# Turning two more attention chunks with VectorE and regrouped data in place of TensorE transposes

## The chip, the cores and the metric

The kernel runs on one core of a Trainium2 chip. The metric is the device time of one execution in microseconds (us); the time before is the median of three runs. All data is fp32.

The core's engines are named as in the profile: PE (TensorE: matmuls and transposes, weight loads shown apart as PEld), DVE (VectorE), ACT (ScalarE), POOL (GpSimd) and SP (SyncE, which here issues nearly all DMA transfers). Each engine runs its own instructions in order and waits on semaphores for the others.

## The reference

Two parts, one behind the other. First a linear attention with decay, on q, k and v of 4 batches x 8 heads x 768 tokens x 64, in blocks of 64 tokens:

```
for b in range(nb):                       # blocks of 64 tokens
    intra = einsum('bhic,bhjc->bhij', qb, kb) * Dmask
    intra = einsum('bhij,bhjd->bhid', intra, vb)
    inter = einsum('bhid,bhde->bhie', qb * lam_pow, kv_state)
    out[block] = intra + inter
    kv_state = lam**64 * kv_state + einsum('bhsd,bhse->bhde', kb * rev_pow, vb)
```

Its output, as 3072 tokens x 512, is the input x of a dense mixture of four experts: `out = sum over e of p[:, e] * (relu(x @ w1[e]) @ w2[e])`, with w1 of 512 x 1024, w2 of 1024 x 512, and p the probabilities of the tokens, normalised.

## The kernel before

**Tiling.** A chunk is 128 tokens of all 8 heads of one batch, so there are 24 chunks; eight make a group, and the three groups of 1024 tokens are the unit of the second part. The products with w1 and w2 are done by a scheme of seven products in place of eight (M1 to M7), partly nested, with sums of operands made by POOL and DVE. A pair (group, expert) is a unit; the twelve units run one behind the other.

**Stages.** At first chunks 0 to 7 go through attention, mixed with the first product of unit (0, 0). Then the main loop runs over the units. Each has seven products, and each product eight places x, so that the work of the loop has a step number, `(at * 7 + i) * 8 + x`. In the part of the trace that matters here a product takes some 13 us, a step some 1.6 us, and step 0 stands at about 87 us. At every step the loop emits some matmuls of the second product of one unit (`q<-w2t,m`, L1254) and of the first product of the next (`pg<-xs,...`, L1195), with the evictions from PSUM to SBUF behind them on DVE (`m<-pg,m`) and ACT (L1208, L1172, L1176); then it takes one or two pieces of deferred work from lists, runs what attention has due at that step, and pumps the chores of POOL (`w1o`, `ops`: the sums for the operands of later products, and their stores).

**Attention in the loop.** Chunks 8 to 23 go through attention in the loop. The schedule is written out by hand: `AT` lists the step at which each chunk's scores are made (34 for chunk 8, 40 for 9, 48 for 10), and `attention()` (L911 and on) derives all other steps from it: the loads, the turn, and `values` of the chunk before.

The scores need q and k turned, with the head dimension on the partitions. There are two ways to it.

- *On PE* (`turn`, L732 and on; chunks 0 to 9): q and k are loaded as they lie, in two half DMAs each (L178); eight PE transposes of 128x128 (L745) put them into two PSUM banks; ACT copies them to SBUF (L753 q, L754 k). The step is 4 before the scores, the load 7 before that.
- *Across* (`turn_across`, from L719; chunks 10 to 23): k is loaded in one DMA (L174), and ACT regroups it in 16 copies of 32x128 (`regroup`, L526), handed out two per step by the list `moves`. q is regrouped in DRAM: `bring_across` (L488) copies it from DRAM to the DRAM tensor `across` in 64 pieces with runs of 128 B, sent one per call of `trickle`, and `load_across` brings one chunk of it to SBUF in one DMA. Two DVE transposes of 128x512 (L725; each turns the 32x32 blocks in place) do the rest. They aren't issued at once, but put in the list `lately`, from which the loop takes at its steps. The turn is 7 steps before the scores, the load of q 5 before the turn, that of k `K_AHEAD` (16 if not listed) before it, and the regrouping 5 or 6 steps behind the load of k.

In both ways POOL then scales k by the decay, in place (`decayed`, `kn<-kn,decay`), and for a later chunk of a batch the state (`begin_state`, `kv<-kv,decay`, L117 as all sums).

`comes_across(n)` decides between the two ways by `FIRST_ACROSS`, and so does the row from which `bring_across` copies a batch: the first chunk of it that needs it.

Of the kernel before, what the change touches and what calls it, by code (L numbers as in the profile page):

```python
# [21 lines left out]
def kernel(  # L22
# [40 lines left out]
    CPG = 8  # L63
# [86 lines left out]
    def where(n):  # L150
        g, x = divmod(n, CPG)
        return (x // 4, x % 4) if g == 0 else (2 * g + x // 2 % 2, 2 * (x // 4) + x % 2)
# [7 lines left out]
    def load(n, names="qkv"):  # L160

        c, b = where(n)
        for name in names:
            x = ({"k": acc_tile, "v": w2_tile} if n < CPG else {}).get(name, small)(f"{name}n")
            src = {"q": q, "k": k, "v": v}[name][b, :, c * C:(c + 1) * C, :]
            if name == "v":
                to, of = x[:].rearrange("p (h d) -> p h d", d=D), src.rearrange("h p d -> p h d")
                for h in (slice(0, 4), slice(4, 8)) if n < CPG else (slice(0, 8),):
                    send(out=to[:, h], in_=of[:, h], by=nc.scalar if n == 0 and h.start else None)
            else:  # L170
                to, of = x[:].rearrange("p (i r d) -> p i r d", r=2, d=D), src.rearrange("(r i) p d -> p i r d", r=2)
                if comes_across(n):
                    to = x[:].rearrange("p (r i d) -> p i r d", r=2, d=D)
                    nc.sync.dma_start(out=x[:].rearrange("p (h d) -> p h d", d=D), in_=src.rearrange("h p d -> p h d"))  # L174
                else:
                    for r in range(2):
                        by = nc.scalar if n == 0 and r == 1 else nc.sync
                        by.dma_start(out=to[:, :, r], in_=of[:, :, r])  # L178
                nat[n, name] = to
                continue  # L180
            nat[n, name] = x[:].rearrange("p (h d) -> p h d", d=D)
# [300 lines left out]

    FIRST_ACROSS = CPG + 2
    across = dram.tile([P, NHP, B, 16, 32], FP32, name="across")
    pieces = []
    rank = {0: 0, 1: 1, 2: 2, 3: 3}  # L488
# [1 line left out]
    def bring_across(b):  # L490
        c = min(where(n)[0] for n in range(FIRST_ACROSS, NG * CPG) if where(n)[1] == b)
        for y in range(4):
            for ac in range(NHP):
                src = q[b, 4 * (y // 2) + ac, c * C:, (y % 2) * 32:(y % 2 + 1) * 32]
                to = across[y * 32:(y + 1) * 32, ac, b, (c - 2) * 4:]
                pieces.append((rank[b], lambda by, to=to, src=src: send(
                    out=to, in_=src.rearrange("(t p) d -> p t d", p=32), by=by,
                )))
# [6 lines left out]
    def comes_across(n):  # L505
        return n >= FIRST_ACROSS

# [10 lines left out]
    def regroup(n):  # L518

        of = nat[n, "k"]  # L520

        def move(j, x):
            if (n, "kx") not in nat:
                nat[n, "kx"] = small("kx")
            to = nat[n, "kx"][:].rearrange("p (h t c) -> p h t c", h=NHP, c=32)
            nc.scalar.copy(  # L526
                out=to[j * 32:(j + 1) * 32, :, x],
                in_=of[x * 32:(x + 1) * 32, :, j // 2, j % 2 * 32:(j % 2 + 1) * 32],
            )

        moves.extend((n, lambda j=j, x=x: move(j, x)) for j in range(4) for x in range(4))
# [5 lines left out]
    def load_more(n):  # L537
        if not comes_across(n):
            load(n, "qk")
        else:  # L540
            trickle(sum(x <= rank[where(n)[1]] for x, _ in pieces))
            load_across(n)
# [156 lines left out]
    def decayed(n):  # L699

        kn = nat[n, "k"]
        kd = kn if n >= CPG else small("kd")[:].rearrange("p (i r d) -> p i r d", r=2, d=D)
        nat[n, "kd"] = kd
        by = k_decay.rearrange("p r ac -> p ac r").unsqueeze(3).to_broadcast([P, NHP, 2, D])
        if comes_across(n):
            kd, kn, by = (x.rearrange("p i r d -> p r i d") for x in (kd, kn, by))
        tt(nc.gpsimd, kd, kn, by, ALU.mult)
# [24 lines left out]
    def turn(n, tags):  # L732
        all_added()
        begin_state(n)
        if comes_across(n):
            turn_across(n)
            return
        if n < CPG:
            decayed(n)
        qn, kn = nat.pop((n, "q")), nat[n, "k"]  # L740
        qp = bank(tags[0], "qp")
        kp = bank(tags[1], "kp")
        for x, y in ((qp, qn), (kp, kn)):
            for ac in range(NHP):
                nc.tensor.transpose(  # L745
                    out=x[:, ac * C:(ac + 1) * C], in_=y[:, ac].rearrange("p r d -> p (r d)"),
                    identity=ident[:],
                )
        if n >= CPG:
            decayed(n)  # L750
        del nat[n, "k"]
        qT, kT = small("qT"), small("kT")
        nc.scalar.copy(out=qT[:], in_=qp[:])  # L753
        nc.scalar.copy(out=kT[:], in_=kp[:])  # L754
        if n >= CPG:
            turned[n] = qT, kT, qT
            return
        qs = small("qs")
        scaled = lambda: scale_q(qs, qp)
        soon(n, scaled)  # L760
        turned[n] = qT, kT, qs, scaled
# [142 lines left out]

    FILL = {1: 18, 2: 43}
    AT = (34, 40, 48, 54, 60, 91, 100, 108, 115, 147, 154, 167, 172, 203, 210, 223)
    K_AHEAD = {10: 14, 11: 14, 12: 15, 14: 17, 15: 18, 16: 18, 18: 17, 20: 19, 22: 17}
    V_AHEAD = {CPG + 10: 8, CPG + 13: 10}
    steps = []

    def attention():  # L911

        first, last = CPG, NG * CPG - 1
        for n in range(first, last + 1):
            s = AT[n - first]
            turns_at = s - (7 if comes_across(n) else 4)

            def both(n=n):
                if n > first:
                    values(n - 1, ("s0", "s1"))  # L920
                scores(n, ("q02", "q12"))

            steps.append((turns_at - (5 if comes_across(n) else 7), lambda n=n: load_more(n)))
            steps.append((s - V_AHEAD.get(n, 7), lambda n=n: load(n, "v")))
            steps.append((turns_at, lambda n=n: turn(n, ("s0", "s1"))))
            if comes_across(n):
                steps.append((turns_at - K_AHEAD.get(n, 16), lambda n=n: load(n, "k")))
                steps.append((turns_at - K_AHEAD.get(n, 16) + (6 if n > CPG + 4 else 5), lambda n=n: regroup(n)))
                steps.append((turns_at, lambda n=n: (decayed(n), nat.pop((n, "k")))))
            steps.append((s, both))  # L930
        steps.append((AT[last - first] + 5, lambda: values(last, ("s0", "s1"))))
        steps.append((AT[last - first] - 14, turn_gates))
        steps.sort(key=lambda s: s[0])
# [911 lines left out]
    def pause_till(i, x):  # L1845
# [17 lines left out]
        "M4": ((("M5", 0),), (("M5", 1),), (("M2", 0),), (("M2", 1),)),  # L1863
    }
    attention()
    PACE = 1.0, 1.0, 1.0
    FEED = (1, 5), (2, 5)
# [154 lines left out]
```

## Time and profile before

| | |
|---|---|
| runs | 1138.53, 1139.07, 1140.1 us; median 1139.07 |
| profiled execution | 1138.78 us, span 1137.0 us, 1.78 us outside the span |
| PE transposes of chunk 8 | start 137.04 us |
| PE transposes of chunk 9 | start 149.56 us |
| scores of chunk 8 (`sp<-qT,kT`) | start 144.91 us |
| ACT evictions of the turned q and k | 137.67 and 138.16; 150.20 and 150.68 us, 0.58 to 0.59 us each |
| POOL decay of chunk 8's k | start 138.16 us, 1.06 us, idle 11.27 us before it |
| pieces to `across`, x8 | SP sends them from 85.77 to 91.72 us |

In a line of a timeline the columns are the start, the time, the engine, the line of the kernel and the operation, the tile written and the tiles read, shapes (partitions x elements), and the count of instructions that the line stands for; a bracket at its end holds the engine's idle time before it and what ended that. The time of a line with several instructions reaches from the first start to the last end. PE's instructions overlap, so that the start of the next tells more of a cost than the time given. In a line of windows the columns are the stretch, its length, then busy time and count for PE, PEld, DVE, ACT and POOL, then PE's granted clock, the DMA share and GB/s.

### The profile page before, as it was taken

The page shows a single profiled execution, that of the slowest core. Times are in us where ns is not written, and L with a number is a line of the kernel's source. Part 1 is how long each engine was busy: PE and PEld are TensorE (multiplying, and loading weights), DVE is VectorE, ACT ScalarE, POOL GpSimd, SP SyncE. Part 2 cuts the span into 40 slices and gives each one's busy share as a digit, 9 for nine tenths or more (in the row PEclk, how much of TensorE's full clock was granted, in tenths as well). Part 3 has the DMA queues.
Part 4 walks back from the last instruction along what each step waited for, and adds up shares of the span by engine and source line. Part 5 has one row for each costly group of instructions (what it writes and reads, how often), then busy time and mean ns, then how long its engine had stood idle before and what let it go on. Part 6 is the DMA issues. An engine that isn't in the chain of part 4 may idle for free.

```text
span 1137.0 us, 22208 instructions
## 1 busy us (share of the span) xinstructions
PE 1128.0 (99%) x7967; PEld 986.1 (87%) x7967; DVE 774.1 (68%) x1478; ACT 445.0 (39%) x988; POOL 764.8 (67%) x730
## 2 busy tenths in 40 slices
PE   8999999999999999999999999999999999999998
PEld 7788888888888888888888888888888888888887
DVE  4576777587587658837655566778767576776785
ACT  4325245255234534422453443344354452342332
POOL 2745547656753976644884998795984873873885
PEclk9999999999999999999999999999999999999999
DMA  9796887889896987876767669876778657656652
GB/s 200 171 281 193 227 223 233 284 273 321 259 361 209 310 270 245 286 270 216 257 195 251 189 197 319 271 225 200 224 231 253 179 161 213 188 159 205 176 195 74
DMA packets 297901, 261.36 MB, mean 230 GB/s; under 512 B 129408, under 2 KB 241216, under 8 KB 297792
## 3 DMA queue, kind: packets, MB, share of 16 engines
q1 hardware_dynamic: 287728, 255.71, 73.0%
q10 hardware_dynamic: 10032, 4.23, 1.5%
q8 instruction: 64, 1.05, 0.4%
q14 instruction: 45, 0.37, 0.1%
q0 software_dynamic: 32, 0.00, 0.0%
HBM read 192.20 MB, written 71.34 MB: 232 GB/s over the span
## 4 chain that ended last, share of the span: by engine, by line
PE 98%; DVE 1%; issue 0%; DMA 0%; ACT 0%; DVEq 0%; POOLq 0%; ACTq 0%
PE pg L1195 41%; PE pq L1571 25%; PE q L1254 21%; PE pM L1713 3%; PE pc L1713 2%; PE op L842 1%; PE sp L779 1%; PE op L860 1%; PE sp L786 1%; PE pM L1438 1%; PE pg L1571 1%; PE qp L745 0%; DMA decay<-in_lam_dram 0%; PE kp L745 0%; DVE m L117 0%
## 5 line engine op out<-in xcount | busy, mean ns | idle before, releaser
L1195 PE MATMUL pg<-xs,ws_in 128*128 128x256 f32 x1960 | 470.1, 380 | 0.1
L1195 PEld LDWEIGHTS pg<-xs,ws_in 128*128 128x128 f32 x1960 | 371.1, 190 | 52.5 <-DVE m L117 2.1
L117 DVE TENSOR_TENSOR m<-pg,m 128x512 f32<-128x512 f32 x374 | 255.3, 685 | 96.9 <-PE pg L1195 87.5
L1254 PE MATMUL q<-w2t,m 128*128 128x256 f32 x1120 | 265.4, 380 | 0.0
L1254 PEld LDWEIGHTS q<-w2t,m 128*128 128x128 f32 x1120 | 212.1, 190 | 29.6 <-issue 0.6
L117 DVE TENSOR_TENSOR sums<-pq,sums 128x256 f32<-128x256 f32 x272 | 112.9, 420 | 90.6 <-PE pq L1571 75.2
L117 POOL TENSOR_TENSOR m<-m,decay 128x512 f32<-128x512 f32 x91 | 114.5, 1271 | 85.9 <-ACT m L1212 64.6
L1571 PE MATMUL pq<-acc,w2t 128*128 128x256 f32 x688 | 169.2, 379 | 0.0
L1571 PEld LDWEIGHTS pq<-acc,w2t 128*128 128x128 f32 x688 | 130.6, 190 | 17.9
L1212 ACT ACTIVATE m<-m 128x512 f32<-128x512 f32 x99 | 62.3, 630 | 154.4 <-DVE m L117 152.3
L117 DVE TENSOR_TENSOR m<-m,m 128x512 f32<-128x512 f32 x108 | 96.9, 898 | 7.8 <-ACT m L1178 7.0
L1208 ACT COPY m<-pg 128x512 f32<-128x512 f32 x88 | 51.5, 586 | 123.4 <-PE pg L1195 115.8
L1272 DVE SCALAR_TENSOR_TENSOR acc<-q,gate,acc 128x256 f32<-128x256 f32 x108 | 52.0, 481 | 69.9 <-PE q L1254 68.9
L1172 ACT COPY pg<-m 128x512 f32<-128x512 f32 x77 | 45.4, 590 | 103.0 <-DVE m L117 88.2
L117 POOL TENSOR_TENSOR acc<-hT,hT 128x512 f32<-128x512 f32 x56 | 70.4, 1271 | 22.6 <-PE pq L1571 13.2
L117 POOL TENSOR_TENSOR acc<-hT,acc 128x512 f32<-128x512 f32 x56 | 71.2, 1272 | 6.5 <-PE pq L1571 2.9
L526 ACT COPY kx<-kn 32x128 f32<-32x128 f32 x224 | 66.2, 295 | 12.8 <-PE op L860 5.1
L1571 PE MATMUL pq<-hT,w2t 128*128 128x256 f32 x288 | 70.0, 379 | 0.0
L117 POOL TENSOR_TENSOR w2o<-w2b 128x512 f32<-128x512 f32 x26 | 35.6, 1391 | 49.2 <-DMA w2b<-in_moe_w_dram 38.2
L1571 PEld LDWEIGHTS pq<-hT,w2t 128*128 128x128 f32 x288 | 54.7, 190 | 7.4
L1176 ACT COPY m<-pg 128x512 f32<-128x512 f32 x44 | 25.7, 585 | 77.0 <-PE pg L1195 70.7
L1571 PE MATMUL pq<-m,w2t 128*128 128x256 f32 x228 | 55.4, 379 | 0.0
(158 smaller groups left out, 1465.2 us busy)
## 6 DMA issues: line engine op xcount, KB each, us to landing
ws_in<-w_ops SPq DMA_DIRECT2D x40, 512.0 KB, 4.8
w2t<-w_ops SPq DMA_DIRECT2D x72, 256.0 KB, 3.1
ws_in<-w_ops SPq DMA_DIRECT2D x60, 256.0 KB, 3.6
ws_in<-w_ops SPq DMA_DIRECT2D x40, 384.0 KB, 3.8
w2b<-in_moe_w_dram SPq DMA_DIRECT2D x56, 256.0 KB, 5.5
w_ops<-ops SPq DMA_DIRECT2D x28, 512.0 KB, 4.7
w_ops<-ops SPq DMA_DIRECT2D x54, 256.0 KB, 3.8
w2t<-w_ops SPq DMA_DIRECT2D x100, 128.0 KB, 2.7
```

What stands on the lines that cost most here:

```text
L117: eng.tensor_tensor(out=o, in0=a, in1=b, op=op)
L526: nc.scalar.copy(out=to[j * 32:(j + 1) * 32, :, x], in_=of[x * 32:(x + 1) * 32, :, j // 2, j % 2 * 32:(j % 2 + 1) * 32],)
L779: nc.tensor.matmul(out=sp[r][half[x], ac * BL:(ac + 1) * BL], lhsT=hc(kT)[half[r], ac, blk[x]], rhs=hc(qT)[half[r], ac, blk[x]], start=(ac ...
L1172: nc.scalar.copy(out=banks[tags[1]][:], in_=new["11"][:])
L1176: nc.scalar.copy(out=o[:], in_=p[:])
L1195: nc.tensor.matmul(out=p[:, j * 256:(j + 1) * 256], lhsT=ws[i][:, j * P:(j + 1) * P], rhs=xs[i], start=(fresh and j == 0), stop=True, skip ...
L1208: nc.scalar.copy(out=new[at][:], in_=p[:])
L1212: nc.scalar.activation(out=new[at][:], in_=new[at][:], func=AF.Relu)
L1254: nc.tensor.matmul(out=p[:, s * DH:(s + 1) * DH], lhsT=h[A_OF[m]][:, c * 256 + s * P:c * 256 + (s + 1) * P], rhs=fed2[g, e, m][uu][:, c], ...
L1272: nc.vector.scalar_tensor_tensor(out=o, in0=x, scalar=w, in1=o, op0=ALU.mult, op1=ALU.add)
L1571: nc.tensor.matmul(out=p[:, 0:256], lhsT=fed3[e, m, i][:, c * P:(c + 1) * P], rhs=b[B_OF[i]][:, c * 256:(c + 1) * 256], start=(fresh and c ...
L1713: nc.tensor.matmul(out=p[:, s * 256:(s + 1) * 256], lhsT=a[c][:, f:f + P], rhs=b[:, c, j * 256:(j + 1) * 256], start=(s == 0 and c == 0 an ...
```

## The change

Three edits. `FIRST_ACROSS` goes from 10 to 8, so that chunks 8 and 9 are turned across as well; no chunk in the loop is then turned by PE, and for the two batches of which these chunks are the first to come, `bring_across` copies 16 rows of blocks where it copied 12 (64 KB per piece instead of 48, for 32 of the 64 pieces). `LEAD` turns chunk 9 at 24 steps before its scores instead of 7, so at step 16; chunk 8 is turned at 7 before, step 27. `K_AHEAD` gets entries of 14 for both: k is loaded at step 2 for chunk 9 and at 13 for chunk 8, regrouped from steps 7 and 18 on, and q is loaded at steps 11 and 22.

```diff
-    FIRST_ACROSS = CPG + 2
+    FIRST_ACROSS = CPG
...
     AT = (34, 40, 48, 54, 60, 91, 100, 108, 115, 147, 154, 167, 172, 203, 210, 223)
-    K_AHEAD = {10: 14, 11: 14, 12: 15, 14: 17, 15: 18, 16: 18, 18: 17, 20: 19, 22: 17}
+    LEAD = {9: 24}
+    K_AHEAD = {8: 14, 9: 14, 10: 14, 11: 14, 12: 15, 14: 17, 15: 18, 16: 18, 18: 17, 20: 19, 22: 17}
...
-            turns_at = s - (7 if comes_across(n) else 4)
+            turns_at = s - (LEAD.get(n, 7) if comes_across(n) else 4)
```

In the program's order PE loses 16 transposes and changes nowhere else. DVE gets four transposes, ACT 32 small copies in place of four evictions. SP sends two loads for each of the two chunks (one of k, one from `across`) instead of four. POOL's decays of the two chunks stand earlier in its queue: that of chunk 9 before the two `w1o` sums that now start at 115.28 us, that of chunk 8 before those that start at 122.46 us. From about 172 us on the order is the same on all engines; the lines below the edit have numbers higher by one.

## Prediction

> **What bounds the kernel now.** I read the page first, then the chain of waits, then the timelines of the stretch that the diff touches (97 to 152 us) engine by engine. TensorE (PE) is busy for 99% of the span, at granted clock 9 (tenths, cut) in all slices, and 98% of the chain that ended last is PE.
>
> ```profile
> PE 1128.0 (99%) x7967; PEld 986.1 (87%) x7967; DVE 774.1 (68%) x1478; ACT 445.0 (39%) x988; POOL 764.8 (67%) x730
> PE 98%; DVE 1%; issue 0%; DMA 0%; ACT 0%; DVEq 0%; POOLq 0%; ACTq 0%
> ```
>
> So time is won only by taking work off PE, and lost only by making PE wait. The windows by stage show where waits could come from: in 111 to 127 us PE has no gap (16.00 of 16.00) while DVE is busy 12.48 and POOL 14.27.
>
> ```profile
> 111.00:127.00 16.00, 16.00 (x76) 14.09 (x75) 12.48 (x19) 2.35 (x4) 14.27 (x13) 1.00 0.89 232
> 127.00:139.00 12.00, 12.00 (x62) 10.61 (x61) 8.22 (x16) 2.82 (x5) 0.84 (x1) 1.00 0.95 221
> ```
>
> (Columns: PE, PEld, DVE, ACT, POOL busy with counts, PE clock, DMA share, GB/s.)
>
> **What is removed from PE.** PE's timeline between 136 and 151 us has the turns of chunks 8 and 9:
>
> ```profile
> 137.04 0.60 PE L745 MATMUL qp<-ident,qn 128*128 128x128 f32 x4
> 137.47 0.60 PE L745 MATMUL kp<-ident,kn 128*128 128x128 f32 x4
> 137.91 1.03 PE L1195 MATMUL pg<-xs,ops 128*128 128x256 f32 x4
> ...
> 149.56 0.60 PE L745 MATMUL qp<-ident,qn 128*128 128x128 f32 x4
> 150.00 0.60 PE L745 MATMUL kp<-ident,kn 128*128 128x128 f32 x4
> 150.44 0.81 PE L1195 MATMUL pg<-xs,ops 128*128 128x256 f32 x3
> ```
>
> The ends overlap, so I take starts: 137.04 to 137.91 and 149.56 to 150.44, 0.87 + 0.88 = 1.75 us for 16 transposes. No idle is shown around them, so all of it is on the path: **-1.75 us**. Nothing else leaves PE or changes its order.
>
> **What DVE gets.** Four transposes of 128x512, a shape that chunks 10 to 23 use now:
>
> ```profile
> L725 DVE STREAM_TRANSPOSE qx<-qx x14: 694/701/711, 167.4 to 476.4; 128x512 f32<-128x512 f32 x14
> ```
>
> 0.70 us each, 2.8 in all. By the program's order, chunk 9's two (step 16) fall behind the pair of evictions at 115.79, at about 117.2 us; chunk 8's two (step 27) stand at about 135.1 and 136.2. The second place has idle DVE time (0.38 before 135.51, 1.04 before 137.24, 1.25 before 138.98): nothing there. The first place is the tight one. DVE then has no idle from 115.19 to 127.6:
>
> ```profile
> 117.20 1.59 DVE L117 TENSOR_TENSOR m<-m,m 128x512 f32<-128x512 f32 x1
> 118.71 0.47 DVE L1268 TENSOR_SCALAR acc<-q,gate 128x256 f32<-128x256 f32 x1
> 119.11 0.81 DVE L117 TENSOR_TENSOR m<-m,m 128x512 f32<-128x512 f32 x1
> 119.84 1.47 DVE L117 TENSOR_TENSOR m<-pg,m 128x512 f32<-128x512 f32 x2
> ...
> 122.97 0.68 DVE L117 TENSOR_TENSOR m<-pg,m 128x512 f32<-128x512 f32 x1
> ```
>
> PE takes a bank again only after its eviction. The one ending at 123.65 (122.97 + 0.68) frees the bank of PE's matmuls at 124.09: 0.44 us to spare; the ones ending at about 120.5 and 127.00 have 0.98 (PE at 121.50) and 0.54 (127.54). Everything behind the transposes is late by 2 x 0.70 = 1.40, changed by what the sum at 117.20 does. That sum takes 0.68 alone and 1.59 here, beside POOL's two sums
>
> ```profile
> 115.28 2.96 POOL L117 TENSOR_TENSOR w1o<-w1b 128x512 f32<-128x512 f32 x2
> ```
>
> It ends 0.55 after they do (118.24, 118.79), so it seems to wait for a POOL instruction under way. [...]
>
> In the new order POOL does the state decay (kv, 0.61 to 1.07 us) and k decay (1.06) of chunk 9 ahead of these sums, so they come 1.67 to 2.13 later: the first ends at 118.43 to 118.89, the second 1.48 after. Our sum is ready at 117.20 + 1.40 = 118.60. If the first is still running, the sum costs 0.29 + 0.55 = 0.84 (0.75 less than now); if the second has just begun, 1.31 + 0.55 = 1.86 (0.27 more). Lateness is 0.65 to 1.67, PE's stall at 124.09 that less 0.44, **+0.21 to +1.23**; the end at 120.5 asks less, and the one at 127.00 comes after PE has been put back by the stall. Neither end is nearer to a row, so I take the middle, +0.72.
>
> **ACT.** Per chunk 16 copies of 32x128 at 0.295 us (L526: 224 copies, 66.2 us) come, 4.7 us, and two evictions of 0.59 (L753, L754) go. ACT has room: for chunk 9 in 98 to 111 us it is busy 6.12 of 13, and evictions that PE needs 1.5 us or more after their end (102.70 to 103.29, needed at 105.09; 107.81 to 108.40, needed at 112.0) are held up by at most the two copies issued per step, 0.6. For chunk 8 the copies fall into
>
> ```profile
> 121.40 0.59 ACT L1172 COPY pg<-m 128x512 f32<-128x512 f32 x1 [7.70 <-DVE m L117]
> ```
>
> and the stretch behind, with 2.35 of 16 us busy. Nothing; if the cover went, 0.6 us per product. The removed evictions at 137.67 and 150.20 had no one waiting on PE.
>
> **POOL.** Its decay of chunk 8's k stood behind the load and PE's turn and held up the queue for 11.27 us (126.9 to 138.16). Now it waits for ACT's last copy (about 128.5), and the operands behind it are ready at about 135 instead of 139.9 to 146.7; PE asks for them at 142.2 at the earliest. Earlier, and no gain, since PE didn't wait. The price may be on DVE: POOL now reads beside the sums of 128 to 135 us, where it was idle. In 139 to 146 the same POOL work costs such sums 1.09, 0.82, 0.70 and 0.68 against 0.68, 0.57 in all; DVE has 1.20 idle before the eviction at 135.51, and the transpose ahead of it takes 0.70: covered at 0.57, 2.3 us of stall if all four went by the 1.59 row. I take 0.
>
> **Waits that are new.** The turn of chunk 9 now needs its k at step 7 and q at step 11. SP's queue is idle between 91.72 and 97.52, so the k load goes there, some 10 us before the first copy. The q load waits for DRAM pieces that land at about 102.0; SP reaches it at 101.9, the operand store behind it lands some 1.3 us later than 107.3, and POOL wants that at 112.16. Two pairs of half loads (121.87 to 124.87, 133.18 to 135.44) leave SP. ACT's first copy for chunk 10 is put behind PE's scores of chunk 8 by the buffers' hand-out (140.7 to about 144.4); they are wanted from 159 on. DVE's masking of chunk 8 stays where it was, with the eviction behind it 0.2 us ahead of PE (151.1, 151.28): at risk only if DVE is late there.
>
> **DMA.** 32 pieces grow from 48 to 64 KB in runs of 128 B: 4096 more packets, 0.52 MB. Cost from 1.6 us (0.52 MB at a rate of 327 GB/s) to 11.8 us (46 ns per packet, from 73.0% of 16 x 1137 us over 287728, on 16 engines), spread over 47 to 99 us. The nearest consumer is the w2t pair that lands at 77.9 and 78.6 and is used at 86.96: 8.4 us to spare, while at most 18 of the 32 pieces (6.6 us by the dear price) stand ahead of it. Nothing.
>
> **Sum.** 1138.78 (the profiled execution: span 1137.0 and 1.78 around it) - 1.75 + 0.72 = 1137.75. That execution is 0.29 under the median of 1139.07, so the median should come to **1138.0**.
>
> **The rivals**, times on the median's scale:
>
> - *Full gain.* POOL lies so that DVE's sum escapes, and later sums too (119.11 at 0.81): stall 0 to 0.2, 1137.3 to 1137.5; if the one real wait behind, 0.3 us of PE on DVE's transpose of chunk 11 at 183.8, goes as well, 1137.0. For it: chunk 10 to 13's transposes stand in busy stretches and only that one made PE wait. Against: slack here is 0.44, less than one transpose.
> - *DVE and POOL collide (slower).* The place is 117 to 124 us, the price that of the 1.59 row: were the four sums ahead of the eviction at 122.97 (now 1.59, 0.81, 0.68, 0.82) all to cost 1.59, lateness would be 1.40 + 2.46 = 3.86, the stall 3.42, and the time 1139.07 - 1.75 + 3.42 = 1140.7; with the 2.3 of the next product, 1143.0. It decides for slower once lateness passes 1.75 + 0.44 = 2.19. For: POOL is 89% busy there. Against: POOL's smaller sums of 128x256 now cost DVE 0.13. [...]
> - *It doesn't do what it says.* PE stops turning, but waits as long for chunk 8's operands (scores at 144.91), so 1139.1. Against: the last transpose ends at about 137, 8 us ahead.
>
> **Numbers.** Forecast 0.52 (1137.5 to 1138.6), full gain 0.20, collision 0.20, no effect 0.08. The range leaves out the far part of the collision and half of the lowest end: 1136.8 to 1140.7. A difference of 0.2% (2.28 us) is about what a measurement of this kernel can tell from none. Faster by more needs under 1136.79, beyond all cases but for the scatter of runs around the full gain (1138.53 to 1140.1 now): 0.12. Slower by more needs over 1141.35, the collision in two products: 0.10. Within: 0.78.
>
> **What would show it.** Right: no L745 behind 100 us, PE's matmuls of 137.91 at 137.04 plus the stall, those of 150.44 at 149.56 - 0.87 plus the stall, a PE gap of 0.2 to 1.2 us near 124 with DVE as releaser, and none elsewhere that is new. DVE sums of over 1.2 us between 128 and 135 would show the collision; a PE wait at the scores of chunks 8 or 9 would show the last rival. A gap near 87 us on w2t would make the DMA term wrong.

## The result

| | before | changed |
|---|---|---|
| median of 8 runs each | 1139.64 us | 1143.41 us |
| lowest and highest | 1138.45, 1140.97 | 1140.84, 1144.09 |
| profiled execution, span | 1138.78, 1137.0 | 1143.53, 1141.8 |

Slower: the ratio is 1.0029, with a 95% interval from 1.0018 to 1.0039. That is 2.1 to 4.4 us more, where the prediction said about 1.0 less, and the median lies over the range given (1136.8 to 1140.7).

The page of the changed kernel looks almost the same; what it shows is the chain, where PE lost three points and DVE, DMA, SP's queue and "issue" have shares of one or two.

```profile
PE 1128.3 (99%) x7951; PEld 983.7 (86%) x7951; DVE 774.8 (68%) x1482; ACT 452.6 (40%) x1016; POOL 765.7 (67%) x730
PE 95%; DVE 2%; DMA 1%; SPq 1%; issue 1%; ACT 0%; DVEq 0%
q8 instruction: 64, 1.05, 0.4%
```

To see where time went, I set each PE instruction of the changed kernel's trace against the same one of before. The difference of starts moves at few places:

| place (us, changed kernel) | the difference moves by | what stands there |
|---|---|---|
| up to 61 | +0.64 | the first stage |
| 122.4 and 125.4 | +0.70 | waits for a DVE eviction |
| 138.4 and 150.0 | -0.87, -0.88 | the removed transposes |
| 174.7 | +1.91 | wait for chunk 10's v |
| 175 to 249 | +0.12 | chunk 11's wait 0.2 shorter, others 0.3 longer |
| 299.4 | +1.40 | a gap without a releaser |
| 330 to 529 | +0.78 | three small waits, drift |

Together +3.8, by which PE's last work comes later; the span has another 0.9 behind it. What the first stage and the end do differs from one execution to the next: at 60 us the twelve other kernels below lay between 1.5 us ahead of before and 2.7 behind. The middle rows are the change's.

The waits of PE, by releaser (columns: total, times, longest):

```profile
PE sp L786 <- DMA vn<-in_v_dram: 1.7, 1, 1.7
...
PE sp L786 <- issue: 1.2, 1, 1.2
...
PE pg L1196 <- DVE m L117: 0.4, 1, 0.4
```

The first line is new: before, PE did not wait for `vn` behind the first stage at all. The last is the stall that was forecast.

PE's timeline shows what was taken off and what was paid. The transposes are gone; the matmuls of 137.91 stand at 138.38, right behind the matmuls that were ahead of the transposes (in the fences a line of dots stands for lines left out):

```profile
136.65 1.89 PE L1255 MATMUL q<-w2t,m 128*128 128x256 f32 x8
138.38 1.03 PE L1196 MATMUL pg<-xs,ops 128*128 128x256 f32 x4
```

and then, in chunk 10's scores and in a later chunk's:

```profile
172.32 0.65 PE L779 MATMUL sp<-qx,kx 64*64 64x64 f32 x32
174.69 0.69 PE L786 MATMUL sp<-vn,kn 64*64 64x64 f32 x32 [1.73 <-DMA vn<-in_v_dram]
...
297.59 0.64 PE L786 MATMUL sp<-vn,kn 64*64 64x64 f32 x31
299.42 0.21 PE L786 MATMUL sp<-vn,kn 64*64 64x64 f32 x1 [1.19 <-issue]
```

In the kernel before, neither place has a gap:

```profile
172.73 0.65 PE L779 MATMUL sp<-qx,kx 64*64 64x64 f32 x32
173.19 0.65 PE L786 MATMUL sp<-vn,kn 64*64 64x64 f32 x32
...
295.97 0.65 PE L786 MATMUL sp<-vn,kn 64*64 64x64 f32 x32
```

The second gap of the changed kernel lies inside a group, before its last of 32 matmuls, so no operand can be what was missing.

Why was v late? SP's timeline of the changed kernel:

```profile
146.63 0.37 SPq L114 DMA_DIRECT2D vn<-in_v_dram  x1
149.36 0.37 SPq L174 DMA_DIRECT2D kn<-in_k_dram  x1
...
160.19 3.86 SPq L114 DMA_DIRECT2D across<-in_q_dram  x1
...
168.65 0.56 SPq L114 DMA_DIRECT2D vn<-in_v_dram  x1
```

and the same transfers in the kernel before:

```profile
145.72 0.37 SPq L114 DMA_DIRECT2D vn<-in_v_dram  x1
146.19 1.63 SPq L174 DMA_DIRECT2D kn<-in_k_dram  x1
...
158.01 3.00 SPq L114 DMA_DIRECT2D across<-in_q_dram  x1
...
165.52 0.55 SPq L114 DMA_DIRECT2D vn<-in_v_dram  x1
```

The load of chunk 11's k (`kn` at 149.36) now has a buffer whose last reader is a PE product that ends at 149.32; before, it was sent at 146.19. SP holds there 2.3 us with a dozen transfers behind it, and the DMA engines run dry (busy share 0.04 in 149 to 150 us). Chunk 10's v is sent at 168.65 instead of 165.52, takes 5.91 us to land instead of 4.07, and lands at 174.56 instead of 169.60, 1.8 us after PE could have begun. So 3.1 us of its delay stand ahead of its sending and 1.8 behind it.

### The profile page after: what moved, and what is told of

Read it like the earlier page. It is cut to its first block, busy times and chain, and to the rows that moved or that the text cites. A ratio compares the mean times of both kernels' runs of the same rounds, so it can differ in the third digit from the quotient of the medians.

```text
span 1141.8 us, 22205 instructions
## 1 busy us (share of the span) xinstructions
PE 1128.3 (99%) x7951; PEld 983.7 (86%) x7951; DVE 774.8 (68%) x1482; ACT 452.6 (40%) x1016; POOL 765.7 (67%) x730
## 4 chain that ended last, share of the span: by engine, by line
PE 95%; DVE 2%; DMA 1%; SPq 1%; issue 1%; ACT 0%; DVEq 0%
PE pg L1196 40%; PE pq L1572 25%; PE q L1255 20%; PE pM L1714 2%; PE pc L1714 2%; DVE m L117 1%; PE op L842 1%; PE sp L779 1%; PE sp L786 1%; PE op L860 1%; DMA kn<-in_k_dram 1%; SPq L114 1%; PE pM L1439 1%; PE pg L1572 1%; DMA vn<-in_v_dram 1%
## 5 line engine op out<-in xcount | busy, mean ns | idle before, releaser
L526 ACT COPY kx<-kn 32x128 f32<-32x128 f32 x256 | 75.6, 295 | 20.1 <-DMA kn<-in_k_dram 5.4
```

The lines of the kernel that those rows point to most:

```text
L526: nc.scalar.copy(out=to[j * 32:(j + 1) * 32, :, x], in_=of[x * 32:(x + 1) * 32, :, j // 2, j % 2 * 32:(j % 2 + 1) * 32],)
```

## The experiments

My theory after the result: three terms of their own. (1) DVE, as forecast. (2) SP, held at chunk 11's k, which comes of chunk 9's early turn, makes chunk 10's v late. (3) The gap at 299 us is PE waiting for its own instructions: the page has 64 transfers of 16 KB on a DMA queue of the kind "instruction" (q8), and PE's 16,442 records in the trace (15,902 weight loads and matmuls, the rest semaphore instructions but for three) make some 257 per transfer. The theory takes them to come in blocks of 256, and 16 transposes fewer to move the borders of the blocks, that is, the places in the program where one block ends and the next begins. The rivals: for (2) the DMA engines, fuller through the larger copies of q; for (3) chance. The blocks are an estimate from these counts; whether PE waits at their borders is what had to be tested.

**The borders of the blocks first.** `e1_pad` is the changed kernel with

```diff
-    warm_small(8)
+    warm_small(24)
```

> The changed kernel with 16 more 64x64 matmuls on zeros at its very start (24 instead of 8), where TensorE waits for its first loads: TensorE's program is as long again as it was before the change, and nothing else differs. Theory (the 1.4 us gap inside the scores of the chunk at 299.4 us is TensorE waiting for its own instructions, because 16 instructions fewer moved the borders of what is fetched at a time): no gap of over 0.5 us without a releaser behind 100 us, and about 1.4 us less than the changed kernel, 1142.0. The wait of 1.9 us for chunk 10's v at 174.7 stays. Rival (that gap is an accident of one execution): time as the changed kernel, 1143.4.

Measured: 1137.8, ratio to before 0.9988 (0.9978 to 0.9997), so some 5 us under the changed kernel. No gap at 296: the same place now reads

```profile
293.56 0.65 PE L779 MATMUL sp<-qx,kx 64*64 64x64 f32 x32
294.02 0.65 PE L786 MATMUL sp<-vn,kn 64*64 64x64 f32 x32
294.60 1.99 PE L1255 MATMUL q<-w2t,m 128*128 128x256 f32 x8
```

The wait for v is still there, but 0.84 instead of 1.9. More went than the theory gave to the gap (5 us where 1.4 was expected), so a control was needed; 2.2 of them stand in the first stage, since at 60 us this trace is 1.5 ahead of before and the changed kernel's 0.6 behind. The program is also not as long again as before, as the expectation has it: a transpose leaves two records in the trace (a weight load and a matmul), a 64x64 matmul on zeros four. The change took 36 of PE's records away (with 4 semaphore instructions), and the padding adds 64.

**The padding in the kernel before** (`e7_b16`, the same edit on before).

> Control of the padding: the kernel before with the same 16 more 64x64 matmuls on zeros at its start. If the padding by itself helps the first stage (a gain that has nothing to do with the change), this is faster than before by about 1.5 us, 1137.7. Theory: TensorE waits for loads there anyway, 1138.5 to 1140, and whether a gap of over 0.5 us without a releaser opens somewhere behind 100 us depends on where the borders of 256 instructions fall; at 296 us none is expected.

Measured: 1138.61, ratio 0.9989 (0.9979 to 0.9999). The padding alone brings 0.1%, just clear of none: in its profile the first stage has 1.0 us of gaps at borders where the kernel before has 1.97 + 0.63 + 1.00. So the padded change and padded before are equal (0.9988 and 0.9989), and padded kernels are to be judged against 0.9989, not against 1.

**The borders put back** (`e12_pad64`): the changed kernel with `warm_small(72)`, a whole block more.

> The changed kernel with 64 more matmuls on zeros at the start, 256 instructions of TensorE, one block: the borders fall where they fall in the changed kernel without padding. Theory (borders of 256 instructions): unlike with 16 more, the gap in the scores near 296 us is back, 1.1 to 2.1 us, ending 1.2 to 1.7 us behind a block's transfer; 1 to 3 us of later start come on top: 1143 to 1147. Rival (any padding cures it, or it is chance): no gap near 296 us.

Measured: 1141.92, ratio 1.0020 (1.0006 to 1.0033), 1.1 us under the range expected, and the gap is back, 2.22 us before the last matmul of the same group, at 298.38:

```profile
295.79 0.58 PE L786 MATMUL sp<-vn,kn 64*64 64x64 f32 x27
298.38 0.21 PE L786 MATMUL sp<-vn,kn 64*64 64x64 f32 x1 [2.01 <-issue]
```

With 16 more it is gone, with 64 more it returns: it hangs on the count, not on chance.

**The same shift in a kernel whose attention is unchanged** (`e7_b48`): before with `warm_small(56)`.

> The kernel before with 48 more 64x64 matmuls on zeros at its start (56 instead of 8). A matmul is four instructions of TensorE here (two weight loads, two passes), so 48 are 192, and the borders of 256 instructions lie where they lie in the changed kernel (64 fewer). Theory (instruction supply): the kernel before, whose attention is not changed, now shows the gap of 1.1 to 2.1 us in the scores near 296 us, without a releaser, and takes 1.4 us or more over the time that its later start costs (up to 2 us), 1141 to 1143. Rival (the gap comes of what the change does to loads and buffers): no gap at 296 us; only the later start, 1139.2 to 1141.

Measured: 1142.61, ratio 1.0025 (1.0015 to 1.0034). The size came as expected, the place didn't: nothing at 296, but gaps of 1.39, 1.19 and 1.02 us (start to start) at 37.6, 43.8 and 49.7, also in groups of 64x64 matmuls and without an operand missing. The counts say why: 48 matmuls are 192 records, 64 short of a block of 256, and the change takes away only 36, so the borders don't lie where the changed kernel has them. Nor does the run show what a mere shift of borders costs: its three gaps make 3.6 us, as do the three that the kernel before has in its first stage (1.97, 0.63, 1.00). Where the 3 us that it takes over the kernel before come from stays open (2.7 of them are there at 60 us).

All gaps of this kind have two marks. The first: a transfer of 16 KB on q8 ends, and PE goes on so much later:

| kernel | gap ends | last q8 transfer ended | later by |
|---|---|---|---|
| changed | 299.42 | 297.91 | 1.51 |
| e2_v10 | 295.93 | 294.55 | 1.38 |
| e3_k11 | 299.81 | 298.50 | 1.31 |
| e5_lead7 | 295.50 | 293.88 | 1.62 |
| e12_pad64 | 298.38 | 296.89 | 1.49 |
| before, first stage | 14.15, 41.25, 46.03 | 12.61, 39.76, 44.59 | 1.54, 1.49, 1.45 |

The second is the place in the program. The fourteen traces have 28 PE gaps of 0.6 us or more (start to start) for which no releaser is found. With PE's recorded weight loads, matmuls and semaphore instructions counted from the start, every one of them stands at number 193 or 194 of a block of 256, and none elsewhere. So where these gaps can stand is not chance.

The border that falls on the group's last matmul at 299.42 in the changed kernel falls into the middle of the same group in the kernel before, at 296.11, and costs nothing there. What differs is the block ahead of it. Less its gap, PE passes it in 1.9 us in the changed kernel, since it holds little but 64x64 matmuls; before, it takes 5.56 us. In the five kernels with the gap it is 1.9 to 2.2. That is not enough by itself: `e7_b48` passes a block in 2.02 us at 451.9 without such a gap.

Of the thirteen traces beside before's, the five with the changed kernel's count of PE instructions (or a block more) have the gap near 296; the other eight don't.

**Chunk 10's v asked for earlier** (`e2_v10`):

```diff
-    V_AHEAD = {CPG + 10: 8, CPG + 13: 10}
+    V_AHEAD = {CPG + 2: 10, CPG + 10: 8, CPG + 13: 10}
```

> The changed kernel with the load of chunk 10's v asked for 3 steps earlier (10 steps ahead of its scores instead of 7), so that it stands ahead of a dozen transfers in SP's queue. Theory (v is late because SP had been held up 3 us earlier by the load of chunk 11's k, which waits for a buffer): the wait at chunk 10's scores (174.7 us, 1.9 us) goes, 1141.5. Rival (the DMA engines are fuller through the larger copies of q, and everything lands later): a wait of 1 us or more stays there, 1142.5 to 1143.4. The gap at 299 us stays in both.

Measured: 1140.79, ratio 1.0014 (1.0004 to 1.0025). No wait at chunk 10's scores: `sp<-vn,kn` follows 0.47 us behind the group ahead of it. The wait is for v alone, and v can be had in time. The gap at 296 stays, 2.05 us, and shows a cost that I had not counted:

```profile
294.00:296.00 2.00, 0.16 (x8) 0.00 (x0) 0.48 (x2) 0.46 (x1) 1.29 (x2) 1.00 0.90 338
296.00:298.00 2.00, 2.00 (x8) 1.65 (x8) 0.00 (x0) 0.00 (x0) 2.00 (x4) 0.76 1.00 380
298.00:300.00 2.00, 2.00 (x6) 1.57 (x5) 1.02 (x3) 0.00 (x0) 1.84 (x4) 0.50 0.77 306
```

The granted clock (third column from the end) falls to 0.50 behind the gap, and the next matmuls lose another 1.69 us against before's.

**Chunk 11's k loaded later**, so that SP isn't held there (`e3_k11`):

```diff
-    K_AHEAD = {8: 14, 9: 14, 10: 14, 11: 14, 12: 15, 14: 17, 15: 18, 16: 18, 18: 17, 20: 19, 22: 17}
+    K_AHEAD = {8: 14, 9: 14, 10: 14, 11: 11, 12: 15, 14: 17, 15: 18, 16: 18, 18: 17, 20: 19, 22: 17}
```

> The changed kernel with the load of chunk 11's k 3 steps later (11 steps ahead of its turn instead of 14), so that SP no longer waits for TensorE at that load with a dozen transfers queued behind it. Theory (that wait is the cause): SP sends the transfers of 150 to 169 us about 2 to 3 us earlier, chunk 10's v is sent by 166 and no wait is left at chunk 10's scores: 1141.5; chunk 11's copies have time to its turn. Rival (DMA engines fuller): the wait stays, 1143.4.

Measured: 1141.16, ratio 1.0022 (1.0008 to 1.0036), and a miss: the wait stays, 1.76 us. SP's queue tells why.

```profile
151.70 2.37 SPq L114 DMA_DIRECT2D w1b<-in_moe_w_dram  x3
154.18 0.58 SPq L114 DMA_DIRECT2D qx<-across  x1
154.87 1.01 SPq L174 DMA_DIRECT2D kn<-in_k_dram  x1
155.94 6.25 SPq L114 DMA_DIRECT2D across<-in_q_dram  x2
...
168.54 0.56 SPq L114 DMA_DIRECT2D vn<-in_v_dram  x1
```

The three `w1b` loads are sent at 151.70 as in before (151.47; changed kernel 153.37), so the hold is gone. But SP then stands 6.25 us at two copies of q, to 162.19, where before it stands 3.00 at one (158.01); the last of the three `w1b` loads ahead has landed at 160.97. v is sent as late as in the changed kernel, and its way takes 6.00 us. So the hold at one load is not the whole cause; it looks as if this stretch is full, and a transfer moved into it comes out at v too.

**A transfer more in the kernel before** (`e11_extra`) tests that; it puts 1.5 MB that nobody reads ahead of chunk 11's k (two lines beside the step that loads k, and a scratch tensor `spill` in DRAM):

```diff
+                    steps.append((turns_at - K_AHEAD.get(n, 16), lambda: nc.sync.dma_start(
+                        out=spill[:].rearrange("p (s f) -> p s f", f=1024),
+                        in_=moe_w1[3, 0:384].rearrange("(s p) f -> p s f", p=P),
+                    )))
```

> The kernel before with one more transfer, 1.5 MB from w1 in DRAM to a scratch tensor in DRAM that nobody reads, sent by SP just ahead of the load of chunk 11's k (146 us). Theory (from 146 to 174 us the DMA engines are full, so that whatever holds up the start of this stretch makes chunk 10's v late by as much; in the kernel before it lands at 169.6 and TensorE asks at 173.2, 3.6 us to spare): 1.5 MB at 327 GB/s are 4.6 us, v lands at about 174.2, and a wait of about 1 us (0.5 to 2) opens at chunk 10's scores in a kernel that has none; 1140.2. Rival (the stretch has slack, and only SP's own waits made v late): v lands under 1.5 us later, no wait there.

Measured: 1142.29, ratio 1.0030 (1.0018 to 1.0043). v lands at 176.04, 6.4 later rather than 4.6, and PE waits 3.14 us at a place where the kernel before has none. The theory's direction and place hold, its size was too small. (The page puts this wait down to POOL's `ops`, which had long been done; the landing of v at 176.04 and PE's start at 176.13 are the pair.) The granted clock is at 0.50 from 175.60 to 182.42, which costs some 3.0 more.

```profile
173.00:176.00 3.00, 0.17 (x12) 0.03 (x4) 0.00 (x0) 2.89 (x12) 2.42 (x4) 0.93 1.03 251
176.00:179.00 3.00, 2.87 (x36) 2.48 (x37) 0.71 (x1) 1.18 (x4) 2.92 (x4) 0.50 1.04 311
179.00:182.00 3.00, 3.00 (x8) 2.36 (x7) 1.68 (x4) 0.00 (x0) 0.98 (x1) 0.50 0.79 298
```

**Which chunk brings what.** Without the early turn of chunk 9 (`e5_lead7`: `LEAD = {}`):

> The changed kernel without the early turn of chunk 9: turned 7 steps ahead of its scores, as chunk 8 and the others. By the buffers' hand-out chunk 11's k then waits for TensorE's scores of chunk 8 (about 146 us), as before the change. Theory: no wait for v at chunk 10's scores (-1.9), no wait for VectorE at 124 us (-0.7), since chunk 9's two transposes fall where VectorE has idle time: 1140.8, or up to 0.5 more if they collide there. The gap at 299 us stays. Rival (DMA engines fuller): the wait for v stays, 1142.7. Rival (turning late makes TensorE wait for chunk 9's operands): a wait at chunk 9's scores near 157 us.

Measured: 1139.55, ratio 0.9998 (0.9986 to 1.0009). No wait at 124 and none at 172; both transposes' gains are there (-0.87 and -0.88); the gap at 295.5 is 1.11 us. That is 1.25 under the expectation, which had taken the two waits off the changed kernel's median; the gap is the shortest of the five here and has no slow clock behind it. Turning chunk 9 no earlier than the others takes off nearly all of the loss. The copies of q are as large here as in the changed kernel, and v lands at 169.57, as before (169.60), so larger copies alone don't make v late.

Chunk 8 alone and chunk 9 alone, each with `warm_small(16)` for its 8 transposes; in both, `bring_across` takes its rows from the chunks that come across:

```diff
     def comes_across(n):
-        return n >= FIRST_ACROSS
+        return n >= FIRST_ACROSS and n != CPG + 1     # e10_only9: n != CPG
```

> The change for chunk 8 alone (chunk 9 is turned by TensorE as before), with 8 more matmuls on zeros at the start in place of its 8 transposes, so that the borders of the instruction blocks stay. Theory (chunk 9's early turn brings the wait for VectorE and the hold of SP at chunk 11's k; chunk 8 brings neither): gain 0.87 in TensorE's start behind 138 us, no wait of over 0.3 us at 124, none at 296, chunk 10's v at most 0.5 late: 1139.2 - 0.9 = 1138.3 or a little under. Rival (the larger copies of q and any turn off TensorE cost DMA time): a wait at chunk 10's scores of 1 us or more.

> The change for chunk 9 alone (chunk 8 is turned by TensorE as before), with 8 more matmuls on zeros at the start. Theory: 0.5 to 0.7 us of waiting for VectorE at 124, SP held at chunk 11's k until about 149 as in the whole change, so that chunk 10's v comes late (TensorE asks 0.9 us later than in the whole change: a wait of 0 to 1 us); gain 0.88; in all 1138.8 to 1140. Rival (the two waits come of both chunks together): no wait at 124 and none at 174, 1138.3.

Measured: chunk 8 alone 1137.55, ratio 0.9982 (0.9973 to 0.9992), with no gap of over 0.3 us between 100 and 182; chunk 9 alone 1138.68, ratio 0.9999 (0.9990 to 1.0008), with both waits:

```profile
171.72 0.65 PE L779 MATMUL sp<-qx,kx 64*64 64x64 f32 x32
172.72 0.69 PE L786 MATMUL sp<-vn,kn 64*64 64x64 f32 x32 [0.36 <-DMA vn<-in_v_dram]
```

and 0.53 us at 123.9. So chunk 9's early turn brings the wait for DVE and the hold of SP (149 us here too), and the two waits, 1.07 in all, eat its 0.88. Chunk 8's turn brings no wait. (With 8 more matmuls before has no run of its own, so that 0.9982 may hold some gain of the padding.)

**Versions without these losses.** The changed kernel with padding and without the early turn (`e8_lead7pad`), and one with padding, chunk 9 turned 26 steps ahead and chunk 10's v loaded 10 ahead (`e8_best26`):

> The changed kernel without the early turn of chunk 9 (7 steps ahead as the others) and with 16 more matmuls on zeros at the start. Theory: no wait for v at chunk 10's scores, none for VectorE at 124 us, no gap at 296 us, so that only the gain of the removed transposes is left: 1139.2 - 1.75 = 1137.5, less what the padding alone may bring at the start. Rival (the gap near 296 us is of chance): 1139.5 as without the padding.

> A version that mends all three: the changed kernel with chunk 9 turned 26 steps ahead (its two VectorE transposes fall into 2.97 us of idle time at 112 us), chunk 10's v loaded 10 steps ahead, and 16 more matmuls on zeros at the start. Theory: none of the three waits is left, about 1137.8 (the changed kernel with padding) - 0.5 - 0.8 = 1136.5. Rival: a wait elsewhere takes their place, 1137.8 or more.

Measured: 1137.07, ratio 0.9981 (0.9971 to 0.9990), and 1137.45, ratio 0.9979 (0.9970 to 0.9989), the second 0.95 over the expectation. Both beat the kernel before and, by the ratios, the change (1.0029); against before with the same padding (0.9989) some 0.1% is left, and the intervals overlap. In `e8_best26` the wait at 123 is down to 0.26 and neither the wait for v nor the gap at 296 is there. `e8_lead7pad` still waits 0.80 us for v, though SP isn't held. So I put the traces side by side, all those in which SP loads k and v in the order of the kernel before (all us):

| kernel | stretch begins (chunk 9's v sent) | SP held at chunk 11's k to | chunk 10's v sent, after the begin | v on its way | v lands | PE waits |
|---|---|---|---|---|---|---|
| before | 145.72 | - | 19.8 | 4.1 | 169.60 | 0 |
| e7_b16 | 144.81 | - | 19.8 | 4.4 | 169.05 | 0 |
| e7_b48 | 148.50 | - | 20.4 | 4.6 | 173.47 | 0 |
| e5_lead7 | 144.63 | - | 20.6 | 4.4 | 169.57 | 0 |
| e10_only8 | 144.85 | - | 20.6 | 4.7 | 170.17 | 0 |
| e8_lead7pad | 144.01 | - | 21.4 | 6.0 | 171.32 | 0.80 |
| changed | 146.63 | 149.36 | 22.0 | 5.9 | 174.56 | 1.91 |
| e1_pad | 144.45 | 147.18 | 21.9 | 4.9 | 171.30 | 0.84 |
| e10_only9 | 146.04 | 148.76 | 21.9 | 4.7 | 172.59 | 0.54 |
| e12_pad64 | 146.67 | 149.39 | 21.0 | 4.4 | 172.10 | 0 |

With the hold v is sent 21.7 us behind the begin on average, without it 20.4; so of a hold of some 2.3 us some 1.3 reach v's sending (the ranges, 21.0 to 22.0 and 19.8 to 21.4, overlap). Its way to landing takes 4.1 to 6.0 us, with the hold or without, and the two longest of the table belong to the changed kernel and to `e8_lead7pad`. So three things use up the 3.6 us that v had to spare: the hold, the faster PE (up to 1.75) and a long way. With the way of 4.1 us that v has in the kernel before, the changed kernel would hardly have waited. That the hold alone makes PE wait is not shown; what makes the way longer or shorter is left open.

## Why the prediction was wrong, point by point

- *-1.75 for the transposes*: right, -0.87 and -0.88 in the changed kernel, -0.87 and -0.88 in `e5_lead7`.
- *DVE, +0.21 to +1.23, taken as +0.72*: right in the place and the size, 0.70 (0.10 at 122.4 and 0.60 at 125.4). But the two transposes don't stand together ahead of the sum, as the working has them; the sum stands between them and met POOL's sums after one. It took 1.33, between the bounds of 0.84 and 1.86. The transposes took 0.70 and 0.69 though POOL was busy beside both (116.96 to 120.92 us). That the total comes so near the middle of the range is in part luck:

```profile
117.83 0.70 DVE L725 STREAM_TRANSPOSE qx<-qx 128x512 f32<-128x512 f32 x1
118.46 1.33 DVE L117 TENSOR_TENSOR m<-m,m 128x512 f32<-128x512 f32 x1
119.72 0.47 DVE L1269 TENSOR_SCALAR acc<-q,gate 128x256 f32<-128x256 f32 x1
120.11 0.69 DVE L725 STREAM_TRANSPOSE kx<-kx 128x512 f32<-128x512 f32 x1
```

- *ACT, POOL, larger pieces at nothing*: right as far as the traces show; no PE wait behind the first stage has ACT's copies or a w2t load as releaser. POOL's operands were ready at 138 and 141 rather than 135, still ahead of PE. The price on DVE that was taken as 0 did appear, and with it the sign named for a collision: two sums take 1.44 and 1.36 where the kernel before has 0.68. It cost PE nothing: its delay against the kernel before stays at 1.34 from 125.6 us to the place of the removed transposes at 138.4:

```profile
131.42 1.44 DVE L117 TENSOR_TENSOR m<-m,m 128x512 f32<-128x512 f32 x1
133.17 1.36 DVE L117 TENSOR_TENSOR m<-m,m 128x512 f32<-128x512 f32 x1
```

- *"Waits that are new"*: the step that failed. The text followed four such waits and left out a fifth, SP at chunk 11's k, though the order of the change puts it there: that load used to wait for PE's scores of chunk 8 and now waits for a product 3 us later. Had its queue been followed, the next thing due was chunk 10's v, with 173.19 - 169.60 = 3.6 us to spare, less the 1.75 that PE gains: 1.8, which is less than the 3.2 us by which the load of k ahead of it is late. Instead the DMA part looked at bytes before 99 us only, though the profile had the DMA engines full later:

```profile
160.00:170.00 10.00, 10.00 (x48) 8.81 (x47) 9.04 (x22) 4.51 (x12) 1.35 (x2) 1.00 1.01 262
```

  (The kernel before; the DMA share is the last but one, 1.01.) The wait for v cost 1.91 in this execution, 0, 0.54 and 0.84 in the three others with the same hold. How long v is on its way, 4.1 to 6.0 us, adds to the hold, and no reading of the order alone could have given that.
- *"Nothing else leaves PE or changes its order"*: the second step that failed; true, and not enough. 36 records fewer moved the borders of PE's blocks of 256 records, which the sum puts at nothing without a word; the gap at one of them cost 1.40 us in this execution, up to 3.9 (2.22 and some 1.7 of slow clock) in others. No rival had this.
- *The rivals*: the slower one put the loss on DVE against POOL with 3.42; the sign was its, the mechanism not. That PE might wait for chunks 8 and 9 themselves was rightly put low: their scores did not wait.
- *The sum*: 1138.78 - 1.75 + 0.70 + 1.91 + 1.40 = 1141.0, and the first stage, the end and small waits of this execution make the 1143.5. The median of 1143.41 holds these scattered parts too; how much of the 8 runs' 3.2 us of spread is the gap near 296 with or without the slow clock behind it stays open, as only one of them was profiled.

## What to carry to other kernels

When an edit moves buffers, list every instruction whose releaser changes, and for a DMA queue follow the transfers behind it to the next one with little to spare (here chunk 10's v, with 3.6 us), through a stretch where the DMA share is near 1 (here 1.01 from 160 to 170 us in the kernel before). Of an edit that adds or drops instructions on the bounding engine, remember what 36 records fewer brought here: a gap of 1.40 us some 150 us behind the last of them, which 64 records more at the start took away and 256 more brought back. Try the same kernel with the count restored by idle work at the start before judging it, and give the kernel before the same padding as a control (here `e7_b16`, 0.9989). Count in the trace's records, not in calls: here a transpose makes two and a 64x64 matmul four, and 16 of these for 16 transposes was no exact return.

## What the runs showed of the hardware

- Near 296 us PE had a gap of 1.1 to 2.2 us, start to start, in five of the fourteen traces (1.11 in `e5_lead7`, 1.40 in the changed kernel, 2.22 in `e12_pad64`), in the middle of a group of 64x64 matmuls, at number 193 or 194 of 256 recorded instructions. The 256 records ahead of the place, nearly all of 64x64 matmuls, pass in 1.9 us in the changed kernel without its gap. In these five PE went on 1.31 to 1.62 us after a 16 KB transfer of q8 had ended, at 41.86 us in the changed kernel 1.24 us after one. That PE waits there for its own instructions is the author's reading of the place, the count and the transfer; no record names what it waits for.
- In this fp32 program a 64x64 matmul leaves two weight loads and two matmuls in the trace (8 calls on zeros, 16 records of each), a 128x128 transpose one of each (7967 matmul records with the 16, 7951 without).
- Behind 100 us, PE gaps of 2.05 (`e2_v10`), 2.11 (`e3_k11`) and 2.22 us (`e12_pad64`) were followed by a granted clock of 0.50 for 3.41 us, which cost some 1.7 more each; one of 3.14 (`e11_extra`) stood beside a spell of 6.82 us that cost some 3.0. After gaps of 1.91 and 1.40 (changed kernel) and 1.76 (`e3_k11`) the trace shows no loss. In the first stage a slow spell followed two shorter gaps close together (1.38 and 1.19 in `e5_lead7`, 1.49 and 1.19 in `e12_pad64`, 1.19 and 1.19 in `e11_extra`), but none followed 1.97 and 1.19 in the kernel before, so these runs show no fixed length of a gap that brings it.
- In twelve of the fourteen traces SP stood 2.3 to 3.9 us at the issue of a copy of q between 156 and 164 us, though the semaphore that it waits for had been raised before (in the kernel before at 154.35, with SP there from 158.01 to 161.01; in the changed kernel SP stood from 160.19 to 164.05). It went on 0.5 to 1.2 us after the last of the three `w1b` loads ahead had landed (0.7 in the kernel before, at 160.35; 0.6 in the changed kernel, at 163.44). What held it is not shown.
